# exp(-ln) on ScalarE in place of VectorE's reciprocal, and a reordered last row tile, in a gated pair of linear-attention blocks

## The chip, the cores and the metric

One core of one Trainium2 chip. The metric is the time of one execution in microseconds (us) of device time; lower is better.

## The reference, cut to what matters

Two linear-attention blocks A and B (2048 rows, 640 columns, 32 heads of 20) work on the same `x` and are mixed by a gate per row:

```python
def _A_ref(x, wqkv, wo):                       # _B_ref is the same with B's weights
    ...
    phi = lambda t: jnp.where(t > 0, t + 1, jnp.exp(t)) + 1e-6
    pq, pk = phi(q), phi(k)
    kv = jnp.einsum("bhsd,bhse->bhde", pk, v)
    z = jnp.einsum("bhsd->bhd", pk)
    num = jnp.einsum("bhqd,bhde->bhqe", pq, kv)
    den = jnp.einsum("bhqd,bhd->bhq", pq, z)[..., None] + 1e-6
    o = num / den
    return ... @ wo

g = _sigmoid((x * gate_w).sum(-1, keepdims=True))
return g * a + (1 - g) * b
```

The change touches `1 / den` and the order of the last rows' output matmuls.

## The kernel before

The kernel is a list of operations, each with an engine and an estimated duration. A list scheduler in the program plans them against each other while the kernel is built, and the order that it plans for each engine is then emitted for good. This is the rule by which it picks, and how it estimates a transfer:

```python
t0 = min(c[0] for c in cand)                                     # earliest possible start on this engine
t, _, o = min(((c[0], c[1], c[2]) for c in cand if c[0] <= t0 + 20.0), key=lambda c: c[1])   # then program order
...
if o.sem is not None:                                            # a DMA
    free[o.eng] = t + 60.0
    dma_free = max(dma_free, t + 1400.0) + o.dur
    end = dma_free + 600.0
```

Queries are made in units of 128 x 512: five matmuls, an exponential on ScalarE ("query exponential"), and two VectorE operations, of which the second ("query sum") writes the query to SBUF:

```python
def q_unit(X, b, k):                 # b: block of 512 rows, k: one of 5 slices of 128 columns
    mms("q%s%d%d" % (X, b, k), ...)                                                  # TensorE
    sch.op("ACT", lambda e: e.activation(ek(), PS[...], ACT.Exp), ...)
    sch.op("DVE", lambda e: e.tensor_scalar(ek(), ek(), 1.0, EPS, op0=ALU.min, op1=ALU.add), ..., name="tq...")
    sch.op("DVE", lambda e: e.scalar_tensor_tensor(out=dst, in0=PS[...], scalar=0.0, in1=ek(), op0=ALU.max, op1=ALU.add), ..., name="sq...")
```

For every pair of blocks, denominator matmuls (`dens`, ten pairs of 128x512) need all query sums of those two blocks. The denominators are inverted, written to DRAM, read back spread over the partitions ("factors"), and the queries are multiplied by them, in place:

```python
def scale_q(b, dtile, pieces):
    sch.op("ACT", lambda e: e.activation(DN[:, ds.slot, :], PS[:, dtile.banks[0], lo : lo + 256], ACT.Identity, bias=EP[:, 0:1]), ..., name="dn%d" % b)
    def rec(e):
        ... return e.reciprocal(RC[:, ds.slot, :], DN[:, ds.slot, :])
    sch.op("DVE", rec, 1740, reads=[(ds,)], writes=[(ds,)], name="rc%d" % b)
    dma("SP", "fw%d" % b, <factor in DRAM>, <RC>, ..., us=0.6)
    dma("SP", "fr%d" % b, <RX>, <factor in DRAM>, ..., us=0.6)
    for j in range(pieces):
        for x, X in enumerate(XS):
            sch.op("DVE", <PQ = PQ * RX>, ..., name="ml%s%d" % (X, b))
```

The program lists, in this order: `queries(0); queries(1); wp_rows("B")` (an 800 KB load of branch B's output weights WPB), `dens(0); scale_q(0); queries(2); queries(3); scale_q(1); dens(2);` and the output row tiles (`final`), with `scale_q(2)` and `scale_q(3)` between them. In `final`, ScalarE scales branch A's product by the gate and VectorE adds branch B's; the last row tile is cut into parts of 320, 160 and 160 columns, and each part does A, then B.

## Time and profile before

| | before |
|---|---|
| time, median of the first 3 runs | 190.69 us (190.65 to 190.99) |
| span in the profile | 189.5 us |
| TensorE (PE) busy | 98% |
| VectorE (DVE) busy | 129.8 us, four reciprocals of 1.744 us among it |

From the profile's page: the span, the busy time of each engine with its share of the span and its instructions, and the chain of work that ended last, by engine:

```profile
span 189.5 us, 3208 instructions
PE 185.9 (98%) x1289; PEld 124.0 (65%) x1289; DVE 129.8 (68%) x275; ACT 76.5 (40%) x129; POOL 8.2 (4%) x14
...
PE 94%; DMA 3%; SPq 1%; issue 0%; ACT 0%; DVE 0%; DVEq 0%; ACTq 0%
```

TensorE is what bounds the kernel: nearly all of the chain is matmuls. Busy time alone would not prove it, as the ends of matmuls are modelled; the starts do. The timeline of TensorE around the second denominators (columns: start and duration in us, engine, line, operation, output<-inputs, partitions x elements, count):

```profile
142.31 1.52 PE L383 MATMUL ps<-WPA,FE 128*128 128x320 bf16 x10
143.67 1.52 PE L383 MATMUL ps<-WPB,FE 128*128 128x320 bf16 x10
145.03 1.52 PE L383 MATMUL ps<-WPA,FE 128*128 128x320 bf16 x10
146.48 0.39 PE L383 MATMUL ps<-FE,ZBDA 128*32 128x512 bf16 x2
...
147.67 1.53 PE L383 MATMUL ps<-WPB,FE 128*128 128x320 bf16 x10
```

The groups of ten output matmuls follow each other by 1.36 us, and the denominators (ZBDA) come 1.45 us after the group ahead of them. Nothing waits. The same stretch on VectorE. L793 is the reciprocal, L811 the multiplies by the factors (the x4 are block 0's, the later ones block 1's), L747 and L752 the two operations of a query unit. In square brackets: the idle time before a line, and what ended it:

```profile
123.48 1.75 DVE L793 RECIPROCAL RC<-DN 128x256 bf16<-128x256 f32 x1
...
125.29 1.74 DVE L793 RECIPROCAL RC<-DN 128x256 bf16<-128x256 f32 x1
...
131.44 3.03 DVE L811 TENSOR_TENSOR FE<-FE,RX 128x1280 bf16<-128x1280 bf16 x4 [0.67 <-DMA RX<-factor]
...
143.99 0.28 DVE L747 TENSOR_SCALAR EK<-EK 128x512 bf16<-128x512 bf16 x1
144.19 0.82 DVE L811 TENSOR_TENSOR FE<-FE,RX 128x1280 bf16<-128x1280 bf16 x1
144.93 0.68 DVE L752 SCALAR_TENSOR_TENSOR FE<-ps,EK 128x512 bf16<-128x512 f32 x1
145.53 2.29 DVE L811 TENSOR_TENSOR FE<-FE,RX 128x1280 bf16<-128x1280 bf16 x3
```

The last query sum (L752 at 144.93) ends at 145.61. TensorE could take its denominators at 146.48, so VectorE has 0.87 us in hand. And the DMA queue (SPq), from its timeline:

```profile
123.36 0.35 SPq L372 DMA_DIRECT2D WPB<-wrowsB  x1
125.26 2.31 SPq L372 DMA_DIRECT2D factor<-RC  x2
128.63 1.38 SPq L372 DMA_DIRECT2D RX<-factor  x2
```

The end of the kernel:

```profile
186.75 0.51 PE L383 MATMUL ps<-WPB,FE 128*128 128x160 bf16 x5
...
187.01 0.39 ACT L859 ACTIVATE TS<-ps,GA 128x160 f32<-128x160 f32 x1 [0.36 <-PE ps L383]
187.51 0.38 DVE L865 SCALAR_TENSOR_TENSOR OL<-ps,GA,TS 128x160 bf16<-128x160 f32 x1 [0.37 <-ACT TS L859]
```

The last part of branch A is scaled by ScalarE (187.01), and VectorE (187.51) waits for that.

### The profile page before, as it was taken

How to read it: one execution, taken by the hardware profiler on the slowest of the kernel's cores; microseconds unless marked ns; L12 is line 12 of the kernel's file. 1: busy time of each engine (PE TensorE's matmuls, PEld its weight loads, DVE VectorE, ACT ScalarE, POOL GpSimd, SP SyncE). 2: the span in 40 equal slices, each digit the busy share in tenths (PEclk: the TensorE clock that was granted, in tenths of full speed). 3: DMA queues.
4: the chain of work that ended last, by engine and by line, in shares of the span. 5: the costliest groups of instructions: out<-in, count | busy, mean ns of one | idle time of the engine just before them, and what ended most of it. 6: DMA issues, size and time to landing. Idle time of an engine off the chain costs nothing.

```text
span 189.5 us, 3208 instructions
## 1 busy us (share of the span) xinstructions
PE 185.9 (98%) x1289; PEld 124.0 (65%) x1289; DVE 129.8 (68%) x275; ACT 76.5 (40%) x129; POOL 8.2 (4%) x14
## 2 busy tenths in 40 slices
PE   7999999999999999999999999999999999999995
PEld 2555555555788888888855666455556677777774
DVE  1398998999600009996179997898999959933324
ACT  2265656565311122103255478565553422332232
POOL 8900000000000000000000000000000000000000
DMA  5999699991011111112143004675000173221212
GB/s 189 298 243 177 211 388 364 337 231 33 0 35 38 35 35 38 35 35 38 35 95 102 5 22 173 166 224 170 0 0 3 44 226 92 86 89 35 73 69 69
DMA packets 31936, 21.49 MB, mean 113 GB/s; under 512 B 16818, under 2 KB 31666, under 8 KB 31922
## 3 DMA queue, kind: packets, MB, share of 16 engines
q1 hardware_dynamic: 31490, 20.80, 39.5%
q10 hardware_dynamic: 432, 0.49, 0.8%
q8 instruction: 10, 0.16, 0.4%
q14 instruction: 4, 0.03, 0.1%
HBM read 12.05 MB, written 5.31 MB: 92 GB/s over the span
## 4 chain that ended last, share of the span: by engine, by line
PE 94%; DMA 3%; SPq 1%; issue 0%; ACT 0%; DVE 0%; DVEq 0%; ACTq 0%
PE ps L383 94%; DMA WK<-in_B_wqkv_dram 3%; SPq L372 1%; ACT TS L859 0%; DVE OL L865 0%; DVEq L276 0%; ACTq L276 0%
## 5 line engine op out<-in xcount | busy, mean ns | idle before, releaser
L383 PE MATMUL ps<-WK,XT 128*128 128x512 bf16 (+2 forms) x250 | 44.0, 337 | 0.5 <-DMA WK<-in_A_wqkv_dram 0.2
L383 PE MATMUL ps<-XN,FE 128*128 128x320 bf16 x320 | 44.3, 300 | 0.0
L383 PEld LDWEIGHTS ps<-XN,FE 128*128 128x128 bf16 x320 | 37.5, 118 | 5.9
L383 PEld LDWEIGHTS ps<-WK,XT 128*128 128x128 bf16 x250 | 24.1, 98 | 20.0 <-DMA WK<-in_A_wqkv_dram 0.5
L743 ACT ACTIVATE EK<-ps 128x512 bf16<-128x512 f32 x40 | 23.9, 597 | 18.5 <-PE ps L383 16.9
L563 ACT ACTIVATE EK<-ps 128x512 bf16<-128x512 f32 (+1 forms) x42 | 21.4, 526 | 16.2 <-PE ps L383 16.2
L752 DVE SCALAR_TENSOR_TENSOR FE<-ps,EK 128x512 bf16<-128x512 f32 x40 | 26.8, 688 | 0.7
L859 ACT ACTIVATE TS<-ps,GA 128x640 f32<-128x640 f32 (+2 forms) x18 | 13.2, 734 | 29.5 <-PE ps L383 29.5
L383 PE MATMUL ps<-WPB,FE 128*128 128x320 bf16 (+1 forms) x165 | 24.7, 295 | 0.0
L383 PE MATMUL ps<-WPA,FE 128*128 128x320 bf16 (+1 forms) x165 | 24.7, 295 | 0.0
L573 DVE SCALAR_TENSOR_TENSOR FE<-ps,EK 128x512 bf16<-128x512 f32 (+1 forms) x42 | 23.9, 596 | 0.5
L865 DVE SCALAR_TENSOR_TENSOR OS<-ps,GA,TS 128x640 bf16<-128x640 f32 x15 | 13.0, 869 | 14.7 <-PE ps L383 14.7
L383 PE MATMUL ps<-XT,WQA 128*128 128x512 bf16 x100 | 22.8, 380 | 0.0
L383 PE MATMUL ps<-XT,WQB 128*128 128x512 bf16 x100 | 22.7, 379 | 0.0
L600 ACT ACTIVATE GS<-ps 128x640 bf16<-128x640 f32 x10 | 7.0, 704 | 37.0 <-PE ps L383 37.0
L383 PEld LDWEIGHTS ps<-WPA,FE 128*128 128x128 bf16 x165 | 15.9, 98 | 6.1
L383 PEld LDWEIGHTS ps<-WPB,FE 128*128 128x128 bf16 x165 | 15.8, 98 | 6.2 <-ACT TS L859 0.4
L383 PEld LDWEIGHTS ps<-XT,WQB 128*128 128x128 bf16 x100 | 11.7, 117 | 9.1
L383 PEld LDWEIGHTS ps<-XT,WQA 128*128 128x128 bf16 x100 | 11.6, 118 | 9.4 <-issue 0.4
L705 DVE SCALAR_TENSOR_TENSOR GP<-XN,GWB 128x640 bf16<-128x640 bf16 x16 | 13.3, 829 | 4.1 <-PE ps L383 3.6
L811 DVE TENSOR_TENSOR FE<-FE,RX 128x1280 bf16<-128x1280 bf16 (+1 forms) x20 | 12.6, 685 | 1.6 <-DMA RX<-factor 1.6
L567 DVE TENSOR_SCALAR EK<-EK 128x512 bf16<-128x512 bf16 (+1 forms) x42 | 11.4, 272 | 3.1
(52 smaller groups left out, 80.3 us busy)
## 6 DMA issues: line engine op xcount, KB each, us to landing
out_dram<-OS SPq DMA_DIRECT2D x15, 160.0 KB, 1.8
XN<-in_A_x_dram SPq DMA_DIRECT2D x3, 640.0 KB, 8.1
factor<-RC SPq DMA_DIRECT2D x4, 256.0 KB, 2.6
RX<-factor SPq DMA_DIRECT2D x4, 256.0 KB, 3.2
WVA<-in_A_wqkv_dram SPq DMA_DIRECT2D x1, 800.0 KB, 10.4
WQA<-in_A_wqkv_dram SPq DMA_DIRECT2D x1, 800.0 KB, 11.9
WVB<-in_B_wqkv_dram SPq DMA_DIRECT2D x1, 800.0 KB, 11.2
WQB<-in_B_wqkv_dram SPq DMA_DIRECT2D x1, 800.0 KB, 12.5
```

The costliest lines, as they stand in the source:

```text
L372: ins = e.dma_start(dst() if callable(dst) else dst, src() if callable(src) else src, transpose=transpose)
L383: ins = pe.matmul(o, l, r, start=a, stop=z, tile_position=tp, skip_group_check=True)
L563: "ACT", lambda e, ps=ps, ek=ek: e.activation(ek(), ps(), ACT.Exp), _act_ns(n), reads=[(tile,)], writes=[(es,)],
L567: "DVE", lambda e, ek=ek: e.tensor_scalar(ek(), ek(), 1.0, EPS, op0=ALU.min, op1=ALU.add), _dve_ns(n, 4),
L573: return e.scalar_tensor_tensor(out=out, in0=two(ps()), scalar=0.0, in1=two(ek()), op0=ALU.max, op1=ALU.add)
L600: "ACT", lambda e: e.activation(GS[:, k, :].rearrange("p (h f) -> p h f", f=HALF), pair(tile, HALF), ACT.Copy),
L705: lambda e, t=t: e.scalar_tensor_tensor(out=GP[:, :], in0=XN[:, t, 0:D], scalar=1.0, in1=GWB[:, :], op0=ALU.mult, op1=ALU.mult, accum_out= ...
L743: "ACT", lambda e: e.activation(ek(), PS[:, tile.banks[0], :], ACT.Exp), _act_ns(512), reads=[(tile,)],
L752: lambda e: e.scalar_tensor_tensor(out=dst, in0=PS[:, tile.banks[0], :], scalar=0.0, in1=ek(), op0=ALU.max, op1=ALU.add),
L811: return e.tensor_tensor(out=v, in0=v, in1=RX[:, xs.slot, 512 * x + w * j : 512 * x + w * j + w].unsqueeze(1).to_broadcast([128, NC, w]), ...
L859: "ACT", lambda e, acc=acc, t_ap=t_ap: e.activation(t_ap(), acc(), ACT.Copy, scale=GA[:, 0, t : t + 1]),
L865: lambda e, acc=acc, t_ap=t_ap, o_ap=o_ap: e.scalar_tensor_tensor(out=o_ap(), in0=acc(), scalar=GA[:, 1, t : t + 1], in1=t_ap(), op0=ALU.m ...
```

## The change

Two things. The reciprocal leaves VectorE: 1 / den becomes exp(-ln(den + eps)) on ScalarE, from one table set that holds both functions, loaded ahead. And in the last row tile, branch A of each part is issued one part ahead, so that ScalarE's scaling is done by the time branch B's matmuls are. The diff, cut to its core:

```diff
+        sch.op("ACT", lambda e: e.preload_act_table_set("natural_log_exp_and_others"), 1300, name="table")
...
-                lambda e: e.activation(DN[...], PS[...], ACT.Identity, bias=EP[:, 0:1]), _act_ns(256),
+                lambda e: e.activation(DN[...], PS[...], ACT.Ln, bias=EP[:, 0:1]), _act_ns(256),
...
-            def rec(e):
-                with nc.allow_low_precision(reason="the factor is a bf16 matmul operand"):
-                    return e.reciprocal(RC[:, ds.slot, :], DN[:, ds.slot, :])
-
-            sch.op("DVE", rec, 1740, reads=[(ds,)], writes=[(ds,)], name="rc%d" % b)
+            sch.op(
+                "ACT", lambda e: e.activation(RC[:, ds.slot, :], DN[:, ds.slot, :], ACT.Exp, scale=-1.0), _act_ns(256, False), reads=[(ds,)],
+                writes=[(ds,)], name="rc%d" % b,
+            )
...
-            for lo, hi in parts:                 # each part: A, then B
+            for i, (lo, hi) in enumerate(parts):
+                if i == 0:
+                    total(0, lo, hi)
+                if i + 1 < len(parts):
+                    total(0, *parts[i + 1])      # A of the next part
+                total(1, lo, hi)                 # B of this part
```

More of the change, by code (lines that the diff above doesn't have):

```diff
@@ L786, in scale_q @@
                 "ACT",
-                lambda e: e.activation(DN[:, ds.slot, :], PS[:, dtile.banks[0], lo : lo + 256], ACT.Identity, bias=EP[:, 0:1]), _act_ns(256),
+                lambda e: e.activation(DN[:, ds.slot, :], PS[:, dtile.banks[0], lo : lo + 256], ACT.Ln, bias=EP[:, 0:1]), _act_ns(256),
                 reads=[(dtile,), ("EP",)], writes=[(ds,)], name="dn%d" % b,
             )
-            def rec(e):
-                with nc.allow_low_precision(reason="the factor is a bf16 matmul operand"):
-                    return e.reciprocal(RC[:, ds.slot, :], DN[:, ds.slot, :])
-            sch.op("DVE", rec, 1740, reads=[(ds,)], writes=[(ds,)], name="rc%d" % b)
+            sch.op(
+                "ACT", lambda e: e.activation(RC[:, ds.slot, :], DN[:, ds.slot, :], ACT.Exp, scale=-1.0), _act_ns(256, False), reads=[(ds,)],
+                writes=[(ds,)], name="rc%d" % b,
+            )
             rep = FD[b].ap()
@@ L826, in final, with total, steps, acc @@
             row = out[0, 128 * t : 128 * t + 128, :]
-            for lo, hi in parts:
+            got = {}
+            def total(x, lo, hi):
                 n = 1 if hi - lo <= 512 else 2
                 w = (hi - lo) // n
-                ts = _Tile(1, ring["ts"])
-                def o_ap(lo=lo, hi=hi, w=w):
+                X = XS[x]
+                tile = _Tile(n)
+                ts = got.setdefault(lo, _Tile(1, ring["ts"]))
+                def steps():
+                    return [
+                        (PS[:, tile.banks[h], 0:w], PQ[X][:, k, 128 * t : 128 * t + 128],
+                         WP[X][:, k, lo + w * h : lo + w * h + w], k == 0, k == NC - 1, None)
+                        for k in range(NC) for h in range(n)
+                    ]
+                def acc():
+                    return PS[:, tile.banks[0] : tile.banks[0] + n, 0:w]
+                def o_ap():
@@ L833, in o_ap, with t_ap @@
                     v = OL[:, lo:hi] if last else OS[:, os.slot, lo:hi]
                     return v.rearrange("p (h f) -> p h f", f=w)
-                def t_ap(ts=ts, hi=hi, lo=lo, w=w):
+                def t_ap():
                     return TS[:, ts.slot, 0 : hi - lo].rearrange("p (h f) -> p h f", f=w)
-                okey = ("OL", lo) if last else (os,)
-                for x, X in enumerate(XS):
-                    tile = _Tile(n)
-                    def steps(X=X, tile=tile, lo=lo, w=w, n=n):
-                        return [
-                            (PS[:, tile.banks[h], 0:w], PQ[X][:, k, 128 * t : 128 * t + 128],
-                             WP[X][:, k, lo + w * h : lo + w * h + w], k == 0, k == NC - 1, None)
-                            for k in range(NC) for h in range(n)
-                        ]
-                    def acc(tile=tile, n=n, w=w):
-                        b0 = tile.banks[0]
-                        return PS[:, b0 : b0 + n, 0:w]
-                    mms(
-                        "f%s%d" % (X, t), steps, [("PQS", X, t)] + [("WP", X, k) for k in range(NC)], [(tile,)], 5 * n * (w + 6),
-                    )
-                    if x == 0:
-                        sch.op(
-                            "ACT", lambda e, acc=acc, t_ap=t_ap: e.activation(t_ap(), acc(), ACT.Copy, scale=GA[:, 0, t : t + 1]),
-                            _act_ns(hi - lo), reads=[(tile,), ("GA",)], writes=[(ts,)], name="fa%d" % t,
-                        )
-                    else:
-                        sch.op(
-                            "DVE",
-                            lambda e, acc=acc, t_ap=t_ap, o_ap=o_ap: e.scalar_tensor_tensor(
-                                out=o_ap(), in0=acc(), scalar=GA[:, 1, t : t + 1], in1=t_ap(), op0=ALU.mult, op1=ALU.add
-                            ),
-                            _dve_ns(hi - lo), reads=[(tile,), (ts,), ("GA",)], writes=[okey], name="fb%d" % t,
-                        )
@@ new lines, in total @@
+                mms("f%s%d" % (X, t), steps, [("PQS", X, t)] + [("WP", X, k) for k in range(NC)], [(tile,)], 5 * n * (w + 6))
+                if x == 0:
+                    sch.op(
+                        "ACT", lambda e: e.activation(t_ap(), acc(), ACT.Copy, scale=GA[:, 0, t : t + 1]), _act_ns(hi - lo),
+                        reads=[(tile,), ("GA",)], writes=[(ts,)], name="fa%d" % t,
+                    )
+                    return
+                sch.op(
+                    "DVE",
+                    lambda e: e.scalar_tensor_tensor(
+                        out=o_ap(), in0=acc(), scalar=GA[:, 1, t : t + 1], in1=t_ap(), op0=ALU.mult, op1=ALU.add
+                    ),
+                    _dve_ns(hi - lo), reads=[(tile,), (ts,), ("GA",)], writes=[("OL", lo) if last else (os,)], name="fb%d" % t,
+                )
@@ L873, in final @@
                         "SP", "out%d_%d" % (t, lo), row[:, p0:hi],
-                        (lambda p0=p0, hi=hi: OL[:, p0:hi]) if last else (lambda: OS[:, os.slot, :]),
+                        (lambda: OL[:, p0:hi]) if last else (lambda: OS[:, os.slot, :]),
                         reads=[("OL", c) for c, _ in parts if p0 <= c < hi] if last else [(os,)], us=0.4,
                     ))
+            for i, (lo, hi) in enumerate(parts):
[4 more added lines that the diff above has]
+                total(1, lo, hi)
         kt = {(X, t): _Tile(2) for X in XS for t in (0, 1)}
```

## The prediction

> **What bounds the kernel.** TensorE. The page has PE busy 185.9 of 189.5 us (98%); the chain of work that ended last is 94% matmuls, one unbroken run from 9.05 to 186.93 us. Busy time can hide stalls, as matmul ends are modelled, so I read the cadence in the timeline: from 149.04 us on, each group of ten 128x320 matmuls starts 1.36 us after the last (136 ns a matmul), through all the finals without one exception; in the query stage five 128x512 matmuls take 1.08 us. The table of waits shows PE waiting 1.4 us in all, every wait in the first 10 us. VectorE is 68% busy, ScalarE 40%.
>
> **What the change removes, adds, moves.**
> - VectorE loses four reciprocals of 1.744 us: 7.0 us.
> - ScalarE gains four Exp of 128x256. A 128x256 Exp out of PSUM took 383 ns; I estimate 0.42 us out of SBUF, 1.7 us in all. Identity with bias (474 ns) becomes Ln with the same bias, same cost. The Trainium skill ("ScalarE: Activation LUTs", What happens when an exp ACTIVATE runs) gives one rate whatever the function; here a Copy (704) and an Exp (703 ns) of 128x640 agree.
> - Table loads: one before (1283 ns at 2.15 us, under the first weights' arrival), one after; the instruction order of the changed kernel has no second. The skill ("Table sets: the hidden batching unit") says that one set holds exp and ln, so switching costs nothing. The load stays right behind ScalarE's three DMA issues; the first Exp is at 7.84 us anyway.
> - Factors are ready some 1.5 to 3 us earlier, so the multiplies by them can start earlier; VectorE's order around them changes.
> - TensorE: same instructions; only the last row tile is reordered.
>
> **How much is on the critical path.** Of the reciprocal part: nothing. In the first place (123 to 127 us) ScalarE is idle 0.48 us in each 1.08 us, so two extra 0.42 us Exps delay the query exponentials by at most some 0.4 us for two units; PSUM has banks in hand. VectorE's backlog there shrinks. In the second (148 to 165 us) the scaled queries were already done at 159.5 and 165.2 us, about 5 and 11 us before TensorE needs them.
>
> Of the tail: a little. Before, the last matmul group of branch A starts at 186.41, ScalarE's scaling of it runs 187.01 to 187.41, VectorE's last sum starts 187.51 and takes 0.38, and the store follows to 189.5. After, ScalarE's part is done before the last B group. But that group still ends where it did: it starts at 186.75, takes 0.34, and VectorE starts about 0.28 us after a group's end (185.99 against 185.72), so at 187.37; VectorE is just then free, too, of the 160-column sum before it (about 187.03 to 187.41). So the last sum starts near 187.40 in place of 187.51: 0.1 us gained, not the 0.5 us of the ScalarE step.
>
> **Predicted:** 190.58 us, range 190.2 to 190.95 (runs of before spread over 0.34 us). Faster by over 2%: 0.005; within 2%: 0.985; slower: 0.01.
>
> **What would show it.** PE busy still about 186 us, groups still 1.36 us apart; VectorE busy about 7 us less (near 122.8), ScalarE about 1.7 more (near 78.2); one table load of 1283 ns; the chain still above 93% PE, its end going from TensorE straight to VectorE without ScalarE; last matmul start to span end shorter by about 0.1 us.
>
> **What would make it wrong.** A further table load in the run; VectorE's new order, with multiplies put before the last query sums, holding up the second group of denominator matmuls (before: sums done at 145.6, matmuls at 146.48; I expect some 0.5 us still in hand); the read of factors queueing behind output stores on the one DMA queue.

## More of the kernel before

The time from issue to landing, in the view of the tile RC (the four factor writes), then in that of WPB:

```profile
DMA to landing us min/median/max: 2.6/2.6/3.4
```

```profile
DMA to landing us min/median/max: 4.5/4.5/4.5
```

The write of the first factors (256 KB) is issued at 125.26, while the 800 KB of WPB are still on their way: issued at 123.36, they land 4.5 us later, at 127.9. Of the four writes the slowest (3.4 us) is this one: the read behind it is issued at 128.63, 0.8 us after WPB has landed.

## The result

| | before | changed |
|---|---|---|
| time, median of 6 runs | 190.67 us (190.61 to 190.99) | 191.80 us (191.40 to 192.04) |
| ratio | | 1.0052 (95% interval 1.0037 to 1.0066) |
| span in the profile | 189.5 us | 190.7 us |

Ratios in this text are the mean time of one kernel's fast runs over that of the other's of the same rounds, so not quite the ratio of the medians quoted. The change costs 1.1 us. It is within 2%, but it is a loss, well clear of the noise, and outside the predicted range.

The page and the chain of the changed kernel:

```profile
span 190.7 us, 3209 instructions
PE 186.9 (98%) x1289; PEld 124.8 (65%) x1289; DVE 124.4 (65%) x271; ACT 77.7 (41%) x133; POOL 8.3 (4%) x14
...
PE 85%; DVE 8%; DMA 4%; ACT 0%; issue 0%; DVEq 0%
```

VectorE is 5.4 us less busy and ScalarE 1.2 us more, yet the chain now runs for 8% through VectorE and for 4% through DMA. Who waited on TensorE (engine, line, waited for: us in total, times, longest), and TensorE's timeline around the second denominators:

```profile
PE ps L383 <- DVE FE L754: 1.0, 2, 0.7
```

```profile
142.44 1.52 PE L383 MATMUL ps<-WPA,FE 128*128 128x320 bf16 x10
144.22 1.52 PE L383 MATMUL ps<-WPB,FE 128*128 128x320 bf16 x10 [0.26 <-DVE FE L754]
145.57 1.52 PE L383 MATMUL ps<-WPA,FE 128*128 128x320 bf16 x10
147.80 0.39 PE L383 MATMUL ps<-FE,ZBDA 128*32 128x512 bf16 x2 [0.70 <-DVE FE L754]
...
148.99 1.53 PE L383 MATMUL ps<-WPB,FE 128*128 128x320 bf16 x10
```

The first group with WPB starts 1.78 us after the one ahead, 0.42 late, and the denominators 2.23 us after theirs (before: 1.45), 0.78 late. Both wait for query sums (L754): the first for the PSUM that they free (in the plan its two banks held query units before), the second for the queries. Together 1.20 us, which is the loss: from the second denominators to the end of the span both kernels take about the same, 43.1 us before and 42.9 after. VectorE (L812 are the multiplies, L754 the query sums):

```profile
132.10 3.03 DVE L812 TENSOR_TENSOR FE<-FE,RX 128x1280 bf16<-128x1280 bf16 x4 [1.78 <-DMA RX<-factor]
...
141.65 0.82 DVE L812 TENSOR_TENSOR FE<-FE,RX 128x1280 bf16<-128x1280 bf16 x1
...
144.79 0.82 DVE L812 TENSOR_TENSOR FE<-FE,RX 128x1280 bf16<-128x1280 bf16 x1
...
146.32 0.82 DVE L812 TENSOR_TENSOR FE<-FE,RX 128x1280 bf16<-128x1280 bf16 x1
147.06 0.68 DVE L754 SCALAR_TENSOR_TENSOR FE<-ps,EK 128x512 bf16<-128x512 f32 x1
```

Two things moved. The multiplies of block 0 start at 132.10, later than before (131.44), though the reciprocal is gone; VectorE stood idle for 1.78 us waiting for the factors. And three of block 1's multiplies (141.65, 144.79, 146.32; 0.74 us of VectorE's time each), not one, now stand ahead of the last query sum, which ends at 147.74 in place of 145.61. The DMA queue:

```profile
123.51 0.35 SPq L372 DMA_DIRECT2D WPB<-wrowsB  x1
124.05 1.69 SPq L372 DMA_DIRECT2D factor<-RC  x2
129.34 1.12 SPq L372 DMA_DIRECT2D RX<-factor  x2
```

The landings of the factor writes, in the view of the tile RC:

```profile
DMA to landing us min/median/max: 2.7/3.8/5.3
```

and that of WPB, in the view of its tile:

```profile
DMA to landing us min/median/max: 5.0/5.0/5.0
```

The factor write is issued 1.2 us earlier (124.05), but it takes 5.3 us in place of 3.4: it is issued 0.5 us behind WPB, and the read is not issued before 129.34, 0.7 us later than before. WPB itself lands later, at 128.5 and not at 127.9, and the read again goes out 0.8 us after that. So the earlier write gained nothing, and the read came later by about as much as WPB landed later. ScalarE, from its groups by form (mean duration after the comma), and the end of the kernel:

```profile
L789 ACT ACTIVATE DN<-ps,EP 128x256 f32<-128x256 f32 x4 | 1.9, 466 | 1.9 <-PE ps L383 1.9
L794 ACT ACTIVATE RC<-DN 128x256 bf16<-128x256 f32 x4 | 1.7, 416 | 0.1
L486 ACT ACT_TABLE_LOAD x1 | 1.3, 1283 | 2.1 <-issue 2.1
```

```profile
187.65 1.42 DVE L863 SCALAR_TENSOR_TENSOR OL<-ps,GA,TS 128x320 bf16<-128x320 f32 x3 [0.79 <-PE ps L383]
...
187.73 0.86 PE L383 MATMUL ps<-WPB,FE 128*128 128x160 bf16 x10
```

Ln costs what Identity cost (466 against 474 ns), Exp 416 ns, and there is one table load. At the end VectorE's three sums follow without ScalarE. From the start of the last 160-column group (187.73 + 0.34 = 188.07) to the end of the span 2.63 us pass, before 2.75: the tail gains 0.1 us.

### The profile page after: what moved, and what is told of

Read it like the earlier page. It is cut to its first block, busy times and chain, and to the rows that moved or that the text cites. A ratio compares the mean times of both kernels' runs of the same rounds, so it can differ in the third digit from the quotient of the medians.

```text
span 190.7 us, 3209 instructions
## 1 busy us (share of the span) xinstructions
PE 186.9 (98%) x1289; PEld 124.8 (65%) x1289; DVE 124.4 (65%) x271; ACT 77.7 (41%) x133; POOL 8.3 (4%) x14
## 4 chain that ended last, share of the span: by engine, by line
PE 85%; DVE 8%; DMA 4%; ACT 0%; issue 0%; DVEq 0%
PE ps L383 85%; DVE FE L754 4%; DMA factor<-RC 3%; DVE FE L812 2%; DMA RX<-factor 1%; DVE EK L749 1%; PE ps L471 1%; DVE OL L863 0%; ACT DN L789 0%; ACT RC L794 0%; DVEq L276 0%
## 5 line engine op out<-in xcount | busy, mean ns | idle before, releaser
L383 PEld LDWEIGHTS ps<-WK,XT 128*128 128x128 bf16 x250 | 24.6, 99 | 19.2 <-issue 0.2
L754 DVE SCALAR_TENSOR_TENSOR FE<-ps,EK 128x512 bf16<-128x512 f32 x40 | 27.2, 691 | 0.9
L812 DVE TENSOR_TENSOR FE<-FE,RX 128x1280 bf16<-128x1280 bf16 (+1 forms) x20 | 12.8, 686 | 3.2 <-DMA RX<-factor 3.2
L749 DVE TENSOR_SCALAR EK<-EK 128x512 bf16<-128x512 bf16 x40 | 11.2, 290 | 4.3 <-ACT EK L745 3.2
```

The source lines that it names most:

```text
L383: ins = pe.matmul(o, l, r, start=a, stop=z, tile_position=tp, skip_group_check=True)
L754: lambda e: e.scalar_tensor_tensor(out=dst, in0=PS[:, tile.banks[0], :], scalar=0.0, in1=ek(), op0=ALU.max, op1=ALU.add),
L812: return e.tensor_tensor(out=v, in0=v, in1=RX[:, xs.slot, 512 * x + w * j : 512 * x + w * j + w].unsqueeze(1).to_broadcast([128, NC, w]), ...
```

## The experiments

Three theories. **A, the order:** the planner, believing the factors early and VectorE free, put two more multiplies ahead of the last query sum, and TensorE pays for them. **B, the late factors:** the write now collides with WPB, so VectorE starts block 0's multiplies later. **C, ScalarE:** Ln and Exp displace the query exponentials. Two smaller rivals: the tail's new order, and the table set.

Five of these runs (e3, e4, e5, e5b, e6) differ from their parent in the order of one engine alone. To get that, the program plans once, edits the lists, and plans again with every engine's order prescribed; the comparison of each built kernel's instruction order with its parent's shows that only the edited engine differs.

```diff
-    def schedule(self):
+    def schedule(self, force=None):
...
                 for o in ready[e]:
+                    if force and e in force and o is not force[e][len(order[e])]:
+                        continue
...
+        deps = {o: dict(o.deps) for o in sch.ops}
         sch.schedule()
+        force = {e: list(v) for e, v in sch.order.items()}
+        ...                                   # dependencies and rings put back, operations looked up by name
+        def behind(e, o, p):
+            force[e].remove(o)
+            force[e].insert(force[e].index(p) + 1, o)
+        <the edit>
+        sch.schedule(force)
```

The profiled runs start their first denominators between 121.20 and 122.27 us, differing already in the first microseconds, so for comparing profiles I count from there. This is the summary; each row is one profile, times in us after the start of the first denominator matmuls, and without any wait the second ones start at 24.82. The runs were made on three chips, each beside the kernel before, whose medians there were 190.52 us (e1 to e4), 190.75 (e5, e6, e7) and 190.84 (e5b, e8, e9, e10); 190.67 belongs to the changed kernel's rounds. So compare kernels by the ratios.

| kernel | inverse on | multiplies ahead of the last sum | block 0's multiplies start | last sum ends | second denominators start | late by | median, us | ratio to before |
|---|---|---|---|---|---|---|---|---|
| before | VectorE | 1 | 9.78 | 23.95 | 24.82 | 0 | 190.67 | |
| changed | ScalarE | 3 | 10.31 | 25.95 | 26.01 | 1.19 | 191.80 | 1.0052 |
| e3_mult_last | ScalarE | 0 | 10.50 | 24.30 | 24.82 | 0 | 190.84 | 1.0003 |
| e4_wpb_behind | ScalarE | 3 | 8.45 | 24.07 | 24.82 | 0 | 190.84 | 1.0008 |
| e6_four_ahead | ScalarE | 4 | 9.55 | 26.19 | 26.24 | 1.42 | 192.37 | 1.0071 |
| e10_both_mended | ScalarE | 0 | 8.45 | 22.73 | 24.82 | 0 | 191.17 | 1.0016 |
| e5_before_order | VectorE | 3 | 9.32 | 24.96 | 25.01 | 0.19 | 191.11 | 1.0006 |
| e5b_order_only | VectorE | 3 | 9.82 | 25.45 | 25.51 | 0.69 | 191.68 | 1.0048 |
| e9_late_only | VectorE | 1 | 10.10 | 24.26 | 24.82 | 0 | 190.64 | 0.9986 |
| e8_order_and_late | VectorE | 3 | 10.42 | 26.05 | 26.11 | 1.29 | 192.08 | 1.0064 |

Where TensorE is late, the second denominators start 0.05 to 0.06 us after the last sum ends; where it is not, the sum was done at least 0.5 us before. e3, e4, e6 and e10 are made from the changed kernel, the e5s, e8 and e9 from the one before.

### The two parts of the change apart: e1_tail_only, e2_recip_only

e1 has the `final` of the changed kernel and the reciprocal of before; e2 the reverse.

```diff
 # e1_tail_only: the changed kernel, less its first part
-        sch.op("ACT", lambda e: e.preload_act_table_set("natural_log_exp_and_others"), 1300, name="table")
-                ... ACT.Ln ... / ACT.Exp, scale=-1.0
+                ... ACT.Identity ... / e.reciprocal(RC, DN)
 # e2_recip_only: the kernel before with those lines the other way round
```

> The kernel before with only the last row tile reordered; the reciprocal stays on VectorE. All theories: TensorE is not held up before the tail, so only the tail's gain of 0.1 us shows: 190.55 us, ratio 0.9993. In the trace, last group of matmuls to end of span 2.63 us (before: 2.75).

> The changed kernel with the last row tile as before: exp and ln only. All theories: the whole loss is here, +1.2 us, 191.9 us, with TensorE waiting 0.4 us before the first branch-B output group and 0.7 to 0.8 us before the second denominators. If the loss were in the tail or in chance at the start, it would be near 190.7.

e1: 190.56 us, ratio 0.9994 (0.9980 to 1.0008); from the first denominators to the end 67.8 us, like before (67.8). The expected 0.1 us is too small for the runs to confirm. In its trace, as in the changed kernel's, VectorE goes on without waiting for ScalarE, and its last sum ends 1.0 us after the start of the last matmul group (before: 1.1). e2: 192.11 us, ratio 1.0071 (1.0057 to 1.0085), 68.95 us from the first denominators (changed: 68.9), with a wait of 0.70 us at the second denominators and the WPB group 0.31 us late. The loss lies in the reciprocal's half.

### The order, mended: e3_mult_last

```diff
+        for m in (named["mlB1"][1], named["mlA1"][1], named["mlB1"][0], named["mlA1"][0]):
+            behind("DVE", m, named["sqB34"][0])
```

> The changed kernel with one edit in VectorE's frozen order: the four multiplies of block 1 stand behind the last query sum, in place of three of them ahead of it. TensorE, ScalarE and the DMA queue keep their order. Theory A (order): VectorE ends its query sums 3 x 0.74 = 2.2 us earlier, at 145.5 in place of 147.75, ahead of the 147.0 that TensorE needs; both waits vanish, 190.55 us. Theory B (late factors alone): the factors still land at 132.1 us, so the waits stay, 191.5 or more. Theory C (ScalarE's Ln and Exp displace the query exponentials): stays at 191.8.

190.84 us, ratio 1.0003 (0.9990 to 1.0016). VectorE in its timeline, then TensorE at the second denominators:

```profile
132.30 3.03 DVE L814 TENSOR_TENSOR FE<-FE,RX 128x1280 bf16<-128x1280 bf16 x4 [1.97 <-DMA RX<-factor]
...
145.41 0.69 DVE L756 SCALAR_TENSOR_TENSOR FE<-ps,EK 128x512 bf16<-128x512 f32 x1
146.02 3.02 DVE L814 TENSOR_TENSOR FE<-FE,RX 128x1280 bf16<-128x1280 bf16 x4
```

```profile
146.62 0.39 PE L385 MATMUL ps<-FE,ZBDA 128*32 128x512 bf16 x2
```

The factors come as late as in the changed kernel, or later (132.30), yet the last sum ends at 146.10 (145.41 + 0.69) and the denominators start at 146.62, 1.45 us after the group ahead of them. Both waits are gone. So late factors alone do not make the loss, and neither do Ln and Exp, which are all still there: theory C falls.

### The factors, early: e4_wpb_behind

```diff
+        for n in ("wpB",):
+            behind("SP", named[n][0], named["fr1"][0])
```

> The changed kernel with one edit in the DMA queue's order: the 800 KB load of branch B's output weights is issued behind the reads of the factors; VectorE keeps the changed order, with three multiplies ahead of the last sum. Theory B: the factor write then lands in 2.6 us in place of 5.3, the factors arrive near 129.8 in place of 132.1, VectorE starts the first multiplies near 130.3 and ends its query sums near 145.9; no wait, 190.55 us. Theory A in its strong form (order alone, whenever the factors come): the waits stay. Both together (a sum of delays against 0.9 us of slack): no wait here and none in e3. Theory C: 191.8.

190.84 us, ratio 1.0008 (0.9996 to 1.0021). The DMA queue's timeline, the landings of the factor writes in the view of the tile RC, and VectorE's timeline:

```profile
124.06 1.69 SPq L374 DMA_DIRECT2D factor<-RC  x2
126.75 1.45 SPq L374 DMA_DIRECT2D RX<-factor  x2
128.30 0.45 SPq L374 DMA_DIRECT2D WPB<-wrowsB  x1
```

```profile
DMA to landing us min/median/max: 2.6/2.6/2.7
```

```profile
130.25 3.02 DVE L814 TENSOR_TENSOR FE<-FE,RX 128x1280 bf16<-128x1280 bf16 x4
...
145.19 0.68 DVE L756 SCALAR_TENSOR_TENSOR FE<-ps,EK 128x512 bf16<-128x512 f32 x1
```

With WPB out of its way the write issued at 124.06 lets the read go out at 126.75, not 129.34. VectorE's order is the bad one, three multiplies ahead, and the last sum still ends at 145.87, in time. So with the factors this early (8.45 in the table, 1.3 us earlier than in the kernel before) the order does not make a loss; with factors as late as in the kernel before it does, as e5b below shows. Early factors are what the prediction had taken for granted, and with them its figure holds: 190.84 us lies in its range.

### The two put into the kernel before: e5_before_order, e5b_order_only, e9_late_only, e8_order_and_late

These keep VectorE's reciprocals, so that the new functions play no part. e5 and e5b are one kernel, run twice on two chips, as its first interval was too wide (one run of the kernel before took 192.03 us in those rounds). The multiplies stand behind the same first operations of a unit as in the changed kernel; some pairs of query operations around them keep the order of the kernel before.

```diff
 # e5, e5b, e8: VectorE's order as in the changed kernel
+        a, b = named["mlA1"], named["mlB1"]
+        for m, u in ((a[0], "B30"), (b[0], "B33"), (a[1], "B34")):
+            behind("DVE", m, named["tq" + u][0])
 # e8, e9: 160 KB more between WPB's load and the factor write
+            if X == "B":
+                dma("SP", "extra", XN[:, 0, 0:D], nat.rearrange("(i k) f -> i k f", k=NC)[:, 0, :], ..., us=0.0)
```

> The kernel before, with VectorE's reciprocals, with one edit: VectorE's order as the changed kernel has it, three multiplies of block 1 ahead of the last query sum in place of one. Theory A (order): two more multiplies of 0.74 us put the last query sum from 145.6 to 147.1 us, TensorE can take it at 146.4, so it waits some 0.6 us: 191.2 us, ratio 1.003. Theories B (late factors) and C (ScalarE's work): neither is in this kernel, so 190.6, ratio 1.000.

> The kernel before with only VectorE's order of the changed kernel, once more, beside the two above on the same chip, as its first interval of 0.998 to 1.003 left it open. Its first profile showed a wait of 0.2 us: 190.9, ratio 1.001. If order alone were the cause: 191.3 or more.

> The kernel before with only the extra 160 KB load, VectorE's order as before. Sum of delays: last query sum near 146.3, just inside what TensorE allows; wait 0 to 0.2 us, 190.7 to 190.8, ratio 1.000. If late factors alone were the cause: 191.3 or more.

> The kernel before (reciprocals on VectorE) with both suspects put in: VectorE's order of the changed kernel, and 160 KB more to load (into a buffer no longer used) between branch B's weights and the factor write on the DMA queue, so that the factors come later, some 0.8 us by the rate at which the 800 KB load went. Sum of delays: last query sum near 147.5, TensorE wants it at 146.4 to 146.5; waits of 0.9 to 1.4 us in the trace, 191.7 us, ratio 1.005 to 1.007. Theory C (ScalarE's Ln and Exp are what costs): they are not in this kernel, 190.7.

Order alone: 191.11 us, ratio 1.0006 (0.9980 to 1.0033), then 191.68 us, ratio 1.0048 (1.0029 to 1.0067); the profiles show 0.19 and 0.69 us of delay. The two profiles differ by when the factors came (9.32 and 9.82 us after the first denominators). The first expectation, 191.2, lies between; the second, 190.9, was too low. TensorE in e5b:

```profile
147.25 0.39 PE L385 MATMUL ps<-FE,ZBDA 128*32 128x512 bf16 x2 [0.62 <-DVE FE L754]
```

By the mark set before it ran (191.3 us or more), e5b shows that the order can cost time by itself: with the factors as late as in the kernel before (9.82 against 9.78), two multiplies more delay TensorE by 0.69 us, and the time is 0.5% longer. Late factors alone: 190.64 us, ratio 0.9986 (0.9968 to 1.0003), no wait. Both: 192.08 us, ratio 1.0064 (1.0045 to 1.0082), and TensorE's waits for query sums are close to those of the changed kernel (1.0, 2, 0.7):

```profile
PE ps L385 <- DVE FE L759: 1.1, 2, 0.9
```

The whole loss can be had without Ln and without the new Exp. In the traces the order alone gives up to 0.69 of these 1.29 us, lateness on top of it the rest; lateness by itself stays within the slack.

### One multiply more: e6_four_ahead

```diff
+        for m in (named["mlB1"][1], named["mlA1"][1], named["mlB1"][0], named["mlA1"][0]):
+            behind("DVE", m, named["tqB34"][0])
```

> The changed kernel with all four multiplies of block 1 just ahead of the last query sum. Sum of delays: the last sum ends another 0.74 us later, near 148.5, so the denominator matmuls start at 148.5 in place of 147.8 and TensorE waits 1.5 us there; the wait of the first branch-B output group (0.4 us in the changed kernel) goes, since the sums ahead of it come earlier. Total 192.1 us, ratio 1.008. If the number of multiplies ahead did not matter, 191.8 as the changed kernel.

192.37 us, ratio 1.0071 (1.0042 to 1.0101). The WPB group starts in time, and the denominators wait 1.34 us: the last sum came at 26.19 in place of 25.95, less than the 0.74 us more that was expected, since in this run block 0's multiplies started 0.76 us earlier (9.55 against 10.31), which takes back about what the fourth multiply added. What is left, 0.24 us, comes from two query units whose two VectorE operations no longer have a multiply between them: they take 0.93 us each in this trace, and 0.80 where operations of two units alternate. The total delay is 1.42 us. The size of the step was missed; the sum of delays holds once this is counted.

### The table set alone: e7_table_only

```diff
 # the kernel before
+        sch.op("ACT", lambda e: e.preload_act_table_set("natural_log_exp_and_others"), 1300, name="table")
```

> The kernel before with the table set that holds exp and ln loaded ahead in place of the compiler's own set, and nothing else. All the profiles of kernels with this set had TensorE start the query stage 0.1 to 0.6 us later than the profiles without; theory D, that the set costs something at the start: 190.8 or more, ratio 1.001. Otherwise[...]: 190.55, ratio 1.000.

190.66 us, ratio 0.9990 (0.9962 to 1.0017), first denominators at 121.25 us, among the earliest. The table set costs nothing that shows.

### Both mended: e10_both_mended

The edits of e3 and e4 together.

> The changed kernel with both mended: the four multiplies behind the last query sum, and branch B's weights loaded behind the reads of the factors. TensorE has no wait, as in either alone; only the tail's 0.1 us is left to gain: 190.55, ratio 0.9995, not clearly faster than before. If VectorE's 7 us were still worth something: below 190.3.

191.17 us, ratio 1.0016 (1.0001 to 1.0032), slower than expected. Its profile has no wait in the stretch at issue (second denominators at 24.82) and 67.7 us from the first denominators to the end, as e3 and e4 have, but the first denominators start at 122.27, the latest of all profiles, with 0.5 us of waits for weight loads in the first microseconds. Why this kernel starts late in all of its runs, if it does, was not tried. No version here is clearly faster than the kernel before: the lowest ratio of a version that keeps part of the change, 0.9990 (e7, the table set alone) or 0.9994 (e1, the tail alone), does not differ from 1.

## Why the prediction was wrong

- **What bounds the kernel: right.** TensorE at full cadence; nothing on VectorE was worth time. e10, where VectorE has 2 us in hand before the second denominators, is no faster for it.
- **Costs of the new operations: right.** Exp 416 ns (0.42 estimated), Ln as Identity, and one table load (1283 ns, as before) with no second. That one set holds both exp and ln is what the Trainium skill ("ScalarE: Activation LUTs", Table sets: the hidden batching unit) lists; the trace agrees. (The rate whatever the function, which the prediction cites from that page, stands there under its next heading, Step-by-step: what each stage is for.) The query exponentials behind them were on time in ScalarE's timeline (the first two after the denominators start at 124.30 and 125.38, 2.51 and 3.59 us after the first denominators; before 2.50 and 3.58). The busy time spared on VectorE was over-rated: 5.4 us and not 7.0, as the other VectorE work took 1.6 us more in sum.
- **The tail: right**, 0.1 us and not the 0.5 us of the ScalarE step.
- **The step that failed: "Factors are ready some 1.5 to 3 us earlier, so the multiplies by them can start earlier."** The inverse was ready 1.2 us earlier for block 0. But the multiplies do not wait for the inverse; they wait for a DMA round trip, and that waits for an 800 KB load ahead of it: in each of the nine profiles with WPB right ahead of the write, the read goes out 0.7 to 0.9 us after WPB has landed, whether the write was issued 0.5 to 0.6 or 1.9 us behind WPB. The multiplies started 0.53 us later (10.31 against 9.78). The kernel before showed this: its first write took 3.4 us where the median was 2.6, and the read went out 0.8 us after WPB had landed (123.36 + 4.5 = 127.9). The Trainium skill ("DMA: Bandwidth & Descriptors", Queues, rings and completion order) says that each DMA engine consumes the descriptors of a queue in ring order; e4 agrees, with 2.6 us for the write with nothing ahead against 5.3 behind WPB.
- **The caveat that came true.** The prediction named VectorE's new order holding up the second denominators, and put "some 0.5 us still in hand". That figure stood on the failed step. The sum, counted from the first denominators: before, the last sum ends at 23.95, 0.87 us before it is needed. Two more multiplies add 2 x 0.735 = 1.47 us, the late start adds 0.53, so 2.00 - 0.87 = 1.13 us of delay; measured 1.19. The 0.53 us are those of one pair of profiles: with WPB right ahead, the multiplies start at 9.55 to 10.50 in four profiles with the inverse on ScalarE (changed, e2, e3, e6) and at 9.32 to 9.82 in five with it on VectorE (before, e1, e5, e5b, e7). So they are mostly later, by 0.5 us in the mean, but not in each. With the factors early as assumed (e4) the slack measured is 0.75 us.
- **Why VectorE's spared time was worth nothing, or less.** It turned into idle time: from 123 to 132 us VectorE was busy for 8.27 us before and for 5.48 us after. Between the denominators and the factors VectorE has only query units, which come at TensorE's pace, so the reciprocals had filled a gap. At 130.3 us it then stands before block 0's multiplies and waits for the factors, though two more query exponentials finish meanwhile (130.35 and 131.43): its order is fixed. From the multiplies on it has no idle time up to the last sum (a query unit takes it 0.80 us, TensorE 1.08, but it starts nearly 5 us behind: at 135.05 it turns to the exponential that was done at 130.35), so every later start and every operation ahead of the last sum goes straight to the end.
- **Where the order came from.** The planner's own times, read out while the kernels are built (no chip is needed), have block 0's factors read 8.23 us after the start of the first denominators in the changed kernel and 8.95 in the one before. The chip's multiplies started at 10.31 and 9.78. The planner saw the change as a gain, found VectorE free near the end of the queries, and filled the holes with multiplies that nobody needed yet; on the chip the holes were not there.

What stays open: block 0's multiplies start up to 0.95 us apart between profiles with the same DMA order (9.55 in e6, 10.50 in e3). Part of it is WPB itself, which takes 4.5 to 5.0 us to land in the four profiles of changed kernels with it ahead and 4.2 to 4.5 us in the five of the kernels made from the one before without the extra load; why it does is not shown. The start of the kernel differs by 1 us. There is one profile of each kernel, and the cause of neither was looked for.

## What to carry to other kernels

Before counting on an earlier result, ask what its consumer really waits for: here a DMA of 256 KB behind one of 800 KB, where an earlier issue only meant a longer wait. Where a planner fixes the order of an engine from estimated durations, a change that is free by itself can move work that is not urgent ahead of work that is; compare the order around each point where the bounding engine takes something over, and sum the delay against the slack measured there. Work that nobody needs soon (here four multiplies) belongs behind the last operation that the bounding engine waits for, whatever the plan says about holes.

## What the Trainium skill lacked or had wrong

- "DMA: Bandwidth & Descriptors" (Queues, rings and completion order) has the rule of ring order but no figure for a smaller transfer behind a larger one: the factor write (256 KB) took 2.6 us with nothing ahead (e4), 3.4 us issued 1.9 us after an 800 KB load (before), and 5.3 us issued 0.5 us after it (changed).
- "ScalarE: Activation LUTs" (What ACT_TABLE_LOAD costs) gives 186 + 0.833 N ns with immediate scale and bias and 280 + 0.833 N with a pointer for bias, so 399 and 493 ns for N = 256; the runs show 410 to 418 ns (Exp, SBUF to SBUF) and 457 to 474 ns (Ln, PSUM to SBUF). So the runs lie 3 to 5% above the page for the first and 4 to 7% below it for the second. Its 1283 ns for a table load is what the trace has.
- No page gives the time of VectorE's reciprocal: 1744 ns for 128x256, f32 to bf16.
- No page says that time taken off an engine that does not bound the kernel can cost time, by the order around it: here 1.1 us lost for 5.4 us of VectorE's busy time saved.
